# Attended blocks turned on VectorE, and Q and K of two chunks by column-tiled products, in an adaLN block with sliding-window attention and a gated MLP

## The chip, the core and the metric

The kernel runs on one core of a Trainium2 chip. The metric is the device time of one execution in microseconds (us). The engines are TensorE (PE in the profile, its weight loads PEld), VectorE (DVE), ScalarE (ACT), GpSimd (POOL) and SyncE (SP), which issues most of the transfers (DMAs).

## The reference

The input x is 2048 rows of 640, all in bf16. Six vectors of 640 come from the condition c; three modulate the attention branch, three the MLP branch. The attention has 32 heads of 20 columns and a causal window of 256 keys. The MLP is gated, with an inner width of 1536.

```python
mod = (_silu(c) @ w_mod).reshape(c.shape[0], 6, 1, -1)
sa, ca, ga, sb, cb, gb = mod[:, 0], ..., mod[:, 5]

def _A_ref(x, wqkv, wo):            # H = 32, Dh = 20, W = 256
    qkv = (x @ wqkv).reshape(B, S, 3, H, Dh).transpose(2, 0, 3, 1, 4)
    q, k, v = qkv[0], qkv[1], qkv[2]
    scores = jnp.einsum('bhqd,bhkd->bhqk', q, k) * Dh ** (-0.5)
    mask = (i - j >= 0) & (i - j < W)
    p = softmax(jnp.where(mask, scores, -1e9))
    o = jnp.einsum('bhqk,bhkd->bhqd', p, v)
    return o.transpose(0, 2, 1, 3).reshape(B, S, D) @ wo

def _B_ref(x, w_gate, w_up, w_down):
    return (sigmoid(x @ w_gate) * (x @ w_up)) @ w_down

h = _layernorm(x) * (1 + ca) + sa
x = x + ga * _A_ref(h, A_wqkv, A_wo)
h = _layernorm(x) * (1 + cb) + sb
x = x + gb * _B_ref(h, B_w_gate, B_w_up, B_w_down)
```

## The kernel before, in words

The 2048 rows are cut into 8 chunks of 256, each of two blocks of 128. Chunk a goes through these stages.

- `ln1` (L874): load x, LN statistics on DVE (`ln_stats`, L773), the inverse root on POOL, scaling; then the block is turned so that its 640 columns lie on the partitions (hT). Chunks 0 and 1 are turned by TensorE with the identity (`pe_transposes`, L831), the others by a transposing DMA (`transp_dma`, L808). Then scale and shift from the modulation (mA, L766) are applied.
- `qkv` (L917): for Q and K of each block, two halves of 320 columns, each a chain of five products (`pe_chain`, L689) of 128 stationary rows' worth of hT and 320 moving columns of the weight, into one of four PSUM buffers M. `evac` (L899) copies a half to a stage tile stg on ACT or DVE, with every head padded from 20 to 32 columns. The stage tile is then turned to QT or KT, in which a group of four heads lies on the 128 partitions: for chunks 0 and 1 (NPQ = 2) by four products with the identity per half and a copy of 512 columns, for the others by a transposing DMA. V is copied without a turn.
- `attention` (L1176): scores, two halves q of 16 heads each. A set of scores fills the single four-bank PSUM tile S; ACT takes exp of its 2048 columns (L1028, L1054, L1091), POOL masks. Chunk 0 has 6 sets, every other chunk 10. `burst` (L1108) multiplies with V; the row sum is a column of V.
- `norm` (L1146) turns the result on DVE in 32x32 blocks (T, L1150), divides by the row sums into Tn (L1157) and turns it back (On, L1159). Then `close` writes On to a DRAM tensor doc with four DMAs per q and reads oT back from it with one, so that the 640 attended columns lie on the partitions without the padding.
- `outproj` (L1221) multiplies oT with wo, adds to x, takes the second LN and turns it by DMA (h2T). `mlp` (L1275) makes gate and up, tanh on ACT, the product on DVE (hh), then down, the residual and the store. The gates ga and gb are folded into wo (L1331) and wd (L1268).

At the start TensorE warms up with products of zeros (L667, L678) while x and the modulation's weights come in; `load_w3` (L627) loads the weights of Q, K, V by column halves, a first piece of wq ahead of everything else.

The order of the work is not left to a run-time scheduler. Every operation is recorded with its engine choice, its reads and writes and a planned duration; `PLAN` (L353) is a list of numbers written out in the source, each of which names one operation and its engine. `schedule` (L151) takes the operations in this order, gives each tile a buffer by planned times, and `emit` writes every engine's list with semaphore waits. An engine executes its list in order: an instruction that waits holds everything behind it on that engine, and SP's list of transfers works in the same way.

## Time and profile before

| what | us |
|---|---|
| median of 3 runs (lowest, highest) | 326.84 (326.5, 327.2) |
| the profiled execution | 326.74 |
| its span, first to last instruction | 324.8 |
| TensorE busy (5044 products) | 316.1 |
| DVE, ACT, POOL busy | 205.6, 213.0, 188.0 |
| granted TensorE clock | 1.0 throughout |

How to read it: a busy share is an average over the whole span, and products overlap in the array, so that "busy" does not say how many a microsecond holds. The windows give the same by stage, the waits say on whom an engine stood still, the timeline gives starts, and the lines of a group give count, busy time, mean duration in ns and idle time ahead of them. A name such as M<-wk,hT says that M is written from wk and hT; buffer numbers are left out. The four PSUM buffers M are shared by all products but the scores.

### The profile page before, as it was taken

The page shows a single profiled execution, that of the slowest core. Times are in us where ns is not written, and L with a number is a line of the kernel's source. Part 1 is how long each engine was busy: PE and PEld are TensorE (multiplying, and loading weights), DVE is VectorE, ACT ScalarE, POOL GpSimd, SP SyncE. Part 2 cuts the span into 40 slices and gives each one's busy share as a digit, 9 for nine tenths or more (in the row PEclk, how much of TensorE's full clock was granted, in tenths as well). Part 3 has the DMA queues.
Part 4 walks back from the last instruction along what each step waited for, and adds up shares of the span by engine and source line. Part 5 has one row for each costly group of instructions (what it writes and reads, how often), then busy time and mean ns, then how long its engine had stood idle before and what let it go on. Part 6 is the DMA issues. An engine that isn't in the chain of part 4 may idle for free.

```text
span 324.8 us, 11997 instructions
## 1 busy us (share of the span) xinstructions
PE 316.1 (97%) x5044; PEld 236.8 (73%) x5045; DVE 205.6 (63%) x426; ACT 213.0 (66%) x228; POOL 188.0 (58%) x349
## 2 busy tenths in 40 slices
PE   6999999989999999999999999999999999999996
PEld 2666767667776777776787777777888777887885
DVE  4699987768686865674755647464845376645423
ACT  2699984788678877988685857676886756320220
POOL 5337858855868677948774846676583958001000
PEclk9999999999999999999999999999999999999999
DMA  7999989998648464726551303465121206112201
GB/s 238 370 315 245 281 161 189 207 192 281 186 91 140 64 139 75 109 60 130 118 71 26 83 2 73 126 65 120 39 47 28 77 22 83 38 46 41 83 0 42
DMA packets 73023, 38.20 MB, mean 118 GB/s; under 512 B 46602, under 2 KB 71690, under 8 KB 72970
## 3 DMA queue, kind: packets, MB, share of 16 engines
q1 hardware_dynamic: 71808, 36.13, 50.6%
q10 hardware_dynamic: 1162, 1.31, 1.5%
q8 instruction: 40, 0.66, 0.9%
q14 instruction: 13, 0.11, 0.1%
HBM read 21.30 MB, written 5.25 MB: 82 GB/s over the span
## 4 chain that ended last, share of the span: by engine, by line
PE 76%; DVE 0%; issue 0%
PE M L686 64%; PE S L687 6%; PE M L687 5%; DVE x L1306 0%
## 5 line engine op out<-in xcount | busy, mean ns | idle before, releaser
L1054 ACT ACTIVATE E<-S 128x2048 bf16<-128x2048 f32 x56 | 105.0, 1876 | 45.7 <-PE S L687 45.4
L1063 POOL TENSOR_SCALAR_AFFINE_SELECT E<-E 128x512 bf16<-128x512 bf16 x112 | 69.6, 635 | 8.4 <-DVE Tn L1157 2.1
L1059 POOL TENSOR_SCALAR_AFFINE_SELECT E<-E 128x256 bf16<-128x256 bf16 x112 | 45.4, 415 | 48.3 <-PE M L686 14.8
L686 PE MATMUL M<-h2T,wu 128*128 128x256 bf16 x480 | 68.0, 273 | 0.5 <-DVE h2T L828 0.5
L686 PE MATMUL M<-h2T,wg 128*128 128x256 bf16 x480 | 67.0, 273 | 0.0
L686 PE MATMUL M<-wd,hh 128*128 128x320 bf16 (+2 forms) x396 | 57.3, 296 | 0.0
L1287 DVE SCALAR_TENSOR_TENSOR hh<-sig,M 128x512 bf16<-128x512 f32 x48 | 32.2, 680 | 34.9 <-ACT sig L1285 24.1
L686 PEld LDWEIGHTS M<-h2T,wu 128*128 128x128 bf16 x480 | 45.3, 98 | 8.4 <-issue 0.7
L686 PEld LDWEIGHTS M<-h2T,wg 128*128 128x128 bf16 x480 | 45.5, 98 | 6.9 <-DVE T L1150 0.2
L686 PEld LDWEIGHTS M<-wd,hh 128*128 128x128 bf16 x396 | 37.0, 98 | 14.0 <-DVE hh L1287 0.2
L1285 ACT ACTIVATE sig<-M 128x512 f32<-128x512 f32 x48 | 28.2, 596 | 27.7 <-PE M L686 27.1
L1032 POOL TENSOR_SCALAR_AFFINE_SELECT E<-E 128x1024 bf16<-128x1024 bf16 x28 | 31.9, 1144 | 6.8 <-DVE st L781 2.5
L1306 DVE TENSOR_TENSOR x<-M,x 128x320 bf16<-128x320 f32 (+2 forms) x33 | 15.7, 479 | 29.4 <-PE M L686 28.9
L687 PE MATMUL S<-QT,KT 20*64 20x256 bf16 (+5 forms) x1856 | 32.3, 228 | 1.3 <-issue 0.7
L687 PEld LDWEIGHTS S<-QT,KT 20*64 20x64 bf16 (+1 forms) x1856 | 20.0, 100 | 18.4 <-issue 8.8
L781 DVE BATCH_NORM_STATS2 st<-x 128x6 f32<-128x320 bf16 x64 | 28.9, 477 | 1.3 <-DMA x<-in_A_x_dram 1.0
L1150 DVE STREAM_TRANSPOSE T<-M 128x512 f32<-128x512 f32 x32 | 21.4, 698 | 13.1 <-PE S L687 10.5
L1028 ACT ACTIVATE E<-S 128x2048 bf16<-128x2048 f32 x14 | 26.3, 1876 | 5.1 <-PE S L687 5.0
L686 PE MATMUL M<-wq,hT 128*128 128x320 bf16 x160 | 25.9, 300 | 1.5 <-ACT hT L827 0.9
L686 PE MATMUL M<-wv,hT 128*128 128x320 bf16 x160 | 26.8, 300 | 0.0
L686 PE MATMUL M<-wk,hT 128*128 128x320 bf16 x160 | 26.2, 300 | 0.0
L686 PE MATMUL M<-wo,oT 128*128 128x320 bf16 x160 | 24.8, 300 | 0.0
(86 smaller groups left out, 362.7 us busy)
## 6 DMA issues: line engine op xcount, KB each, us to landing
x<-in_A_x_dram SPq DMA_DIRECT2D x19, 160.0 KB, 8.4
doc<-On SPq DMA_DIRECT2D x64, 40.0 KB
out_dram<-x SPq DMA_DIRECT2D x14, 160.0 KB, 1.8
wd<-in_w_mod_dram SPq DMA_DIRECT2D x6, 320.0 KB
wd<-in_B_w_down_dram SPq DMA_DIRECT2D x4, 480.0 KB
wu<-in_w_mod_dram SPq DMA_DIRECT2D x5, 320.0 KB
oT<-doc SPq DMA_DIRECT2D x8, 192.0 KB
wg<-in_B_w_gate_dram SPq DMA_DIRECT2D x2, 576.0 KB
```

Source lines behind the costliest of these rows:

```text
L686: return e.matmul(o, l, r, start=st, stop=sp, skip_group_check=True)
L687: return e.matmul(o, l, r, start=st, stop=sp, tile_position=tp, skip_group_check=True)
L781: A("dve", lambda e, g, bi=bi, j=j: e.bn_stats(v(bi * 12 + j * 6, 6), src[bi].ap[:, j * 320:(j + 1) * 320]), 0.48, reads=[src[bi].r()], wr ...
L1028: A("act", lambda e, eng: e.activation(cell().rearrange("p m (x c) -> p m x c", c=64)[:, :, 0:4:3, :], Sp.ap[:].rearrange("p j (k x c) -> ...
L1032: A("pool", lambda e, eng, c0=c0, pat=pat, base=base, cm=cm: e.affine_select(cell()[:, :, c0:c0 + 64], cell()[:, :, c0:c0 + 64], pattern=p ...
L1054: A("act", lambda e, eng: e.activation(part(0, 512), Sp.ap[:], ACT.Exp, scale=SM_SCALE), 1.876, reads=[Sp.r()], writes=[E.r("C"), E.r("B") ...
L1059: A("pool", lambda e, eng, hc=hc, src=src, far_h=far_h: e.affine_select(side(hc), part(src, 64), pattern=[[0, 4], [-1 if far_h else 1, 64] ...
L1063: A("pool", lambda e, eng, c0=c0, near=near: e.affine_select(part(c0, 128), part(c0, 128), pattern=[[0, 4], [1 if near else -1, 128]], com ...
L1150: A("dve", lambda e, g, h=h: e.transpose(T1.ap[:, 512 * h:512 * h + 512], X[h].ap), 0.694, reads=[X[h].r()], writes=[T1.r(h)], prio=3.5, t ...
L1285: A("act", lambda e, g, pg=pg, sg=sg: e.activation(sg.ap[:], pg.ap[:], ACT.Tanh, scale=0.5), c_act(512), reads=[pg.r()], writes=[sg.r()], ...
L1287: A("dve", lambda e, g, pu=pu, sg=sg, f0=f0: e.scalar_tensor_tensor(out=hh.ap[:, f0:f0 + 2, :], in0=sg.ap[:].rearrange("p (a b) -> p a b", ...
L1306: A("dve", lambda e, g, ps=ps, bi=bi, c0=c0, n=n: e.tensor_tensor(x1[bi].ap[:, c0:c0 + n], ps.ap[:, 0:n], x1[bi].ap[:, c0:c0 + n], op=ALU. ...
```

## The change

1. Attended blocks: doc and its DMAs are gone. Tn is one tile per chunk of 1280 columns without padding (and without its memset on POOL); `norm` divides straight into it, and after the second q two turns on DVE of 640 columns each give oT. This needs another order of heads on the partitions: head 8j + gi where it was 4 gi + j, so wo is loaded with its rows permuted, in five DMAs of one row tile each, and scaled tile by tile.
2. Q and K of chunks 0 and 1: `qk_turned`. hT is the stationary side in pieces of 32 tokens, the weight moves in four pieces of 160 columns side by side in the four column groups of the array. The half is evacuated with padding, and one DVE turn of 128x1024 in 32x32 blocks gives QT or KT. The products with the identity and the copies of 512 columns are gone. The chain of five is cut 1 + 2 + 2.
3. The weights of Q, K, V are loaded by row tiles (1 + 2 + 2 for wq, 3 + 2 for wk and wv) of all 640 columns, behind x and the modulation's weights; chunk 1's x comes between them.
4. A new `PLAN`. Among other things the Q, K and V products of chunk 0 stand together ahead of the first scores, and the first MLP stands further ahead. For the other chunks only the head order changes in the evacuation of Q and K.

Helpers for paired buffers that were switched off (`both`, `both_banks`, PAIR, TR1, PQ) are removed.

```diff
-    p_Tn = sbpool("Tn", 1, [128, 1024])
-    p_On = sbpool("On", 1, [128, 1024])
+    p_Tn = sbpool("Tn", 1, [128, 1280])
...
-    def load_w3(k, prio, halves):
...
+    def load_rows(k, t0, t1, prio):
         i = ("wq", "wk", "wv").index(k)
...
+        dma(lambda: W3[k][:, t0:t1, :], lambda: wqkv_src[:, t0:t1, i * D:i * D + D], 0.44 * (t1 - t0),
+            writes=R_row[k][t0:t1], prio=prio, tag=k)
...
-    dma(lambda: wo[:], lambda: A_wo.rearrange("(t p) f -> p t f", p=128), 2.15, writes=[R_wo], prio=0.5, tag="wo")
+    for t in range(NDT):
+        dma(lambda t=t: wo[:, t, :], lambda t=t: A_wo.rearrange("(j e) f -> j e f", j=4)[:, 32 * t:32 * t + 32, :], 0.43, writes=[R_wo[t]],
+            prio=0.5, tag="wo")
...
+    def qk_turned(a, prio, bi, key, w, dst, s):
+        for half in range(2):
+            ps = Tile(p_M, f"{key}{a}_{bi}{half}")
+            for t0, t1 in CUTS:
+                def fn(e, g, t0=t0, t1=t1, half=half, ps=ps):
+                    for kt in range(t0, t1):
+                        for i in range(2):
+                            k0 = bi * 128 + (2 * half + i) * 32
+                            for j in range(4):
+                                ins = mm(e, ps.ap[32 * j:32 * j + 32, i * 160:i * 160 + 160], hT[a].ap[:, kt, k0:k0 + 32],
+                                         W3[w][:, kt, j * 160:j * 160 + 160], kt == 0 and i == 0, kt == NDT - 1, tp=(0, 32 * j))
+                    return ins
...
+            evac(lambda half=half: s.ap[:].rearrange("p (m b x) -> p b m x", b=4, x=32)[:, 2 * half:2 * half + 2, :, 0:DH],
+                 lambda ps=ps: ps.ap[:, 0:320].rearrange("p (b m d) -> p b m d", b=2, d=DH), 320, [ps.r()], [s.r(half)], 6, f"evqk{a}")
+        A("dve", lambda e, g: e.transpose(dst.ap[:, :, bi * 128:bi * 128 + 128], s.ap[:]), 1.24, reads=[s.r(0), s.r(1)],
+          writes=[dst.r((bi, 0)), dst.r((bi, 1))], prio=5, tag=f"qtr{a}")
...
-                if a < NPQ or (a, key, bi) in PQ:
-                    for half in range(2):
-                        ps = Tile(p_M, "qtr")
...
-                                ins = mm(e, ps.ap[:, i * 128:i * 128 + 128], s.ap[:, gi * 128:gi * 128 + 128], ident[:],
-                                         i == 0, True)
...
-        A("dve", lambda e, g: e.transpose(On.ap[:], Tn.ap[:]), 1.22, reads=[Tn.r()], writes=[On.r()], prio=4, tag=f"tr2_{a}")
+        A("dve", lambda e, g: e.tensor_tensor(
+            Tn.ap[:].rearrange("p (b k d) -> p k b d", k=8, d=DH)[:, 4 * q:4 * q + 4],
+            T1.ap[:].rearrange("p (k b r) -> p k b r", k=4, r=32)[:, :, :, 0:DH],
+            Dr.ap[:].rearrange("p (k b) -> p k b", k=4).unsqueeze(3).to_broadcast([128, 4, 8, DH]), op=ALU.mult),
...
-            for j in range(4):
-                Rj = R(f"doc{a}_{q}_{j}")
-                dma(lambda j=j, q=q: rdoc[j * DH:(j + 1) * DH, 4 * q:4 * q + 4, :],
...
             if q == 1:
+                for bi in range(2):
+                    A("dve", lambda e, g, bi=bi: e.transpose(
+                        oT.ap[:, :, bi * 128:bi * 128 + 128].rearrange("p t (b c) -> p b t c", c=32), Tn.ap[:, 640 * bi:640 * bi + 640]),
+                      0.83, reads=[Tn.r(0), Tn.r(1)], writes=[oT.r(bi)], prio=4, tag=f"tr2_{a}")
                 x1, h2 = outproj(a, oT)
                 mlp(a, x1, h2)
```

130 lines of the change are left out of this document (44 added, 86 removed), and 223 rows, old and new, of the table PLAN.

## The prediction

> **What bounds the kernel now.** I read the page first: busy shares, then the two lines on transfers.
>
> ```profile
> PE 316.1 (97%) x5044; PEld 236.8 (73%) x5045; DVE 205.6 (63%) x426; ACT 213.0 (66%) x228; POOL 188.0 (58%) x349
> DMA  7999989998648464726551303465121206112201
> GB/s 238 370 315 245 281 161 189 207 192 281 186 91 140 64 139 75 109 60 130 118 71 26 83 2 73 126 65 120 39 47 28 77 22 83 38 46 41 83 0 42
> ```
>
> TensorE is busy in 97% of the span and no other engine in more than 66%. The transfers are dense only in the first ten slices, about 80 us. Next come the windows by stage (columns: busy us and count of PE, weight loads, DVE, ACT, POOL; clock; transfer share; GB/s), which say where TensorE is not busy.
>
> ```profile
> 10.00:20.00 10.00, 9.30 (x98) 6.54 (x98) 7.95 (x21) 7.68 (x15) 2.96 (x10) 1.00 1.06 372
> 20.00:30.00 10.00, 9.98 (x173) 6.62 (x172) 9.13 (x25) 9.67 (x10) 7.31 (x12) 1.00 1.05 260
> 30.00:40.00 10.00, 9.73 (x202) 7.20 (x200) 9.35 (x18) 9.42 (x13) 8.35 (x12) 1.00 0.97 266
> 40.00:60.00 20.00, 19.25 (x334) 13.22 (x333) 16.32 (x39) 13.77 (x17) 14.97 (x28) 1.00 1.02 193
> 60.00:80.00 20.00, 18.33 (x328) 13.06 (x326) 14.98 (x33) 16.53 (x20) 11.72 (x21) 1.00 1.09 221
> 200.00:300.00 100.00, 100.00 (x1555) 78.16 (x1553) 56.76 (x108) 56.10 (x53) 53.46 (x97) 1.00 0.33 64
> ```
>
> Between 10 and 80 us TensorE idles 0.70 + 0.02 + 0.27 + 0.75 + 1.67 = 3.41 us; from 80 us on it is always fed, as the last row shows. So from 80 us on only fewer or cheaper TensorE instructions shorten the run, and before that idle time of at most 3.4 us and the start can be won too. But between 20 and 40 us DVE and ACT are over 90% busy: what is put on them there is not free. The waits of TensorE (us in total, times, longest) name who ends that idle time.
>
> ```profile
> PE M L686 <- DVE x L803: 1.3, 1, 1.3
> ...
> PE M L686 <- ACT hT L827: 0.9, 1, 0.9
> PE S L687 <- issue: 0.7, 1, 0.7
> PE M L686 <- DVE h2T L828: 0.5, 1, 0.5
> PE M L686 <- DVE hT L820: 0.5, 1, 0.5
> ```
>
> The reader is to see that no wait on oT, the attended block that comes back from DRAM, is among them. That detour is hidden under other products, so its removal by itself gives TensorE nothing.
>
> **The change part by part.** TensorE's price of an instruction is its distance to the next start, not its modelled duration. These rows of the timeline (start, us, engine, operation) give it:
>
> ```profile
> 25.82 0.67 PEld L687 LDWEIGHTS M<-wu,silubc 128*32 128x32 bf16 x40 [0.21 <-issue]
> 25.83 0.87 PE L687 MATMUL M<-wu,silubc 128*32 128x160 bf16 x40
> 26.63 0.85 PE L686 MATMUL M<-wq,hT 128*128 128x320 bf16 x5
> ...
> 29.08 0.40 PE L686 MATMUL M<-ident,stg 128*128 128x128 bf16 x4
> 29.31 0.84 PE L686 MATMUL M<-wq,hT 128*128 128x320 bf16 x5
> 29.99 0.39 PE L686 MATMUL M<-ident,stg 128*128 128x128 bf16 x4
> 30.31 0.40 PE L687 MATMUL S<-QT,KT 20*128 20x128 bf16 x16
> 30.64 1.53 PE L686 MATMUL M<-wk,hT 128*128 128x320 bf16 x10
> 32.01 0.44 PE L686 MATMUL M<-wv,hT 128*128 128x320 bf16 x2
> ```
>
> *Transposes gone.* Four of them take 29.31 - 29.08 = 0.23 us, 57 ns each. The group row counts 64:
>
> ```profile
> L686 PE MATMUL M<-ident,stg 128*128 128x128 bf16 x64 | 5.6, 220 | 0.0
> ```
>
> All 64 are Q and K of chunks 0 and 1, and all go: 64 x 57 ns = **-3.65 us**.
>
> *Q and K as column-tiled products.* Before: 2 chunks x 2 blocks x 2 (Q, K) x 2 halves x 5 = 80 products of 320 columns, each (32.01 - 30.64) / 10 = 137 ns, 10.96 us. After: each becomes 2 x 4 products of 32 stationary and 160 moving columns, 640 in all. The same form stands at 25.83: 40 of them in 0.80 us, 20 ns each, of which one change of the array's tiling is part. That change costs (30.31 - 29.99) - 0.23 = 0.09 us, so 0.71 / 40 = 17.8 ns, times 640 = 11.4 us: **+0.4 us**. Bounds: at the column rate of the 320-column products, four side by side would take 160 / 320 x 137 = 68.5 ns, 10.96 us in all, so 0; at the full 20 ns it is 12.8 us, +1.85. I take the value of the row itself.
> The Trainium skill, "TensorE: Matmul & The Clock Gate", section "LDWEIGHTS (loading the stationary operand)", gives a load as its columns divided by 1.2 ns. For 32 columns that is an estimate of 27 ns; were every load in line, 640 would make 17.1 us, and the sum would be 5.7 us worse, about 329 us. The trace speaks against it: 40 loads and 40 products together passed in 0.80 us.
>
> *Changes of tiling.* Counting in the two built orders, TensorE changes tiling 170 times before and 175 after (transposes no longer break scores from products, but tiled products stand among 128-wide ones): 5 x 0.09 = **+0.5 us**.
>
> *The start.* At present a 240 KB piece of wq is issued ahead of x and of the five pieces of the modulation; afterwards it stands behind them. These rows are the queue's first issue, the size of that piece, the copy of the finished modulation and the first projection:
>
> ```profile
> 0.79 0.45 SPq L576 DMA_DIRECT2D wq<-in_A_wqkv_dram  x1
> ...
> 10.43 0.17 DVE L766 COPY mA<-S 128x10 f32<-128x10 f32 x1 [1.42 <-PE S L686]
> ...
> 11.32 2.70 PE L686 MATMUL M<-wq,hT 128*128 128x320 bf16 x17 [0.49 <-DVE hT L820]
> ```
>
> ```profile
> wq<-in_A_wqkv_dram SPq DMA_DIRECT2D x1, 240.0 KB
> ```
>
> 240 KB at the 370 GB/s of the second slice are 0.66 us, so modulation and first projection come **0.65 us** sooner (10.65 us). Bounds: 0, if wq's first row then lands last, and 1.1, if the 0.45 us of issue count as well.
>
> *The idle time between 10 and 80 us.* It goes where it is and comes elsewhere. The order is new, so I look for places at which the new one has to wait. One row of scores needs the single S tile, which exp gives back:
>
> ```profile
> 18.61 1.88 ACT L1091 ACTIVATE E<-S 128x2048 bf16<-128x2048 f32 x1
> ...
> 21.01 1.88 ACT L1091 ACTIVATE E<-S 128x2048 bf16<-128x2048 f32 x1
> ...
> 23.44 1.88 ACT L1091 ACTIVATE E<-S 128x2048 bf16<-128x2048 f32 x1
> ```
>
> So sets of scores cannot follow each other faster than every 2.4 us. In the new order there are only 1.4 us of TensorE work between the first and the second set (ten transposes of x, 16 tiled products): 1.0 us of waiting. Rows 3 and 4 of wq: at present 2.21 MB are in some 0.2 us ahead of the copy at 10.43; 2.79 MB, which these rows end, are there 0.58 / 0.37 = 1.6 us later, at 11.8, and TensorE wants them at 10.65 + 0.7: 0.4 us. The products of K find the four buffers of Q still being emptied, all by ACT: 0.4 us. Two later pairs of sets stand 2.0 and 2.2 us apart: 0.6 us. And the first MLP is brought forward: 46.6 us of TensorE work after the first projection where it was 58.0, behind 15 sets of scores instead of 18. It waits for wo, the residual, LN statistics and h2T's turn by DMA:
>
> ```profile
> h2T<-x SPq DMA_TRANSPOSE x16, 5.1
> ```
>
> From the last product of wo (37.4 us into the new order) the adds, statistics and scaling take some 4 us of DVE and POOL, the turn 5.1, the modulation 0.6: 47.1 to 48, so about 1 us late. Together 1.0 + 0.4 + 0.4 + 0.6 + 1.0 = 3.4 us, as much as the 3.41 that is there now: **0**, between -2.4 (all but 1 us goes) and +2.5.
>
> *DVE, ACT and queues.* Rows of DVE's turns, and of the copies that vanish with the transposes:
>
> ```profile
> L1150 DVE STREAM_TRANSPOSE T<-M 128x512 f32<-128x512 f32 x32 | 21.4, 698 | 13.1 <-PE S L687 10.5 <-PE M L687 2.3
> L1159 DVE STREAM_TRANSPOSE On<-Tn 128x1024 bf16<-128x1024 bf16 x16 | 19.9, 1242 | 0.4
> L903 DVE CAST QT<-M 128x512 bf16<-128x512 f32 x5 | 3.4, 683 | 0.3 <-PE M L686 0.3
> L903 DVE CAST KT<-M 128x512 bf16<-128x512 f32 x3 | 2.1, 685 | 0.2 <-PE M L686 0.2
> ```
>
> ```profile
> L902 ACT ACTIVATE KT<-M 128x512 bf16<-128x512 f32 x5 | 3.0, 599 | 0.1
> L902 ACT ACTIVATE QT<-M 128x512 bf16<-128x512 f32 x3 | 1.8, 595 | 0.0
> ```
>
> DVE gets 8 turns of 128x1024, 9.9 us, and loses 5.5 us of copies; ACT loses 4.8. The closing turn shrinks from 1024 to 640 columns, by the first two rows (1.06 ns a column) to 0.83 us, 16 x 0.41 = 6.5 us less, but spread over the run. So in the first 40 us DVE carries 4.4 us more; the order answers by giving ACT the copies of chunk 0. I cost it at nothing on the path, hidden by TensorE's own 8 us of chunk 0 products; if that cover fails, the first scores come late, which is the first rival. The new wait that matters there: DVE's statistics of x2 and x3 stop for their landing (3.77 and 4.42 MB, by the same count about 14.4 and 16.2 us), and behind them stands the turn of K's first block, on which the first set of scores waits; it ends near 18.7, TensorE gets there near 19.7. The 64 writes and 16 reads of the detour leave SP's queue and the transfers; wo comes in 5 row pieces instead of one, the memset of Tn goes. None of these ended a wait of TensorE above: 0.
>
> **Sum.** -3.65 + 0.4 + 0.5 - 0.65 + 0 = -3.4 us. The profiled execution took 326.74 us (324.8 span and 1.94 around it), 0.1 below the median of 326.84; against the median 323.4 us.
>
> **The rivals.**
> 1. *The first 45 us are not TensorE's.* If the chain of copies, turns and exps on ACT and DVE sets the pace there, the 3.65 us of transposes turn into waiting and only the start is won: 326.84 - 0.65 = 326.2, from 325.2 to 327. For it: the 9.1 to 9.7 us of 10 on DVE and ACT. Against: TensorE idles just 0.29 us between 20 and 40 us, and work that it does not do there it does later, always fed. 0.20.
> 2. *The idle time goes.* The MLP's products, available 11 us of work earlier, and a freer queue fill the gaps: 2.4 us less, 321.0. 0.15.
> 3. *Slower: TensorE's instructions don't arrive.* The row
>
> ```profile
> q8 instruction: 40, 0.66, 0.9%
> ```
>
> says 40 fetches for 10089 instructions of TensorE, 252 each, of 0.9% x 16 x 324.8 / 40 = 1.17 us. Now 20 to 40 us needs 747 instructions in 20 us, 37 per us; the tiled Q and K of chunk 0 are 320 products and 320 loads in 5.7 us without a break, one fetch every 2.25 us, while the transfers are saturated. If a fetch may only run one ahead and takes as long as the turn of h2T above (5.1 us), chunk 0 waits 2.5 x 2.85 = 7.1 us: 330.5. The gain of 3.4 us is used up from 2.25 + 3.4 / 2.5 = 3.6 us per fetch on. 0.06.
> The Trainium skill, "Runtime: NRT & Kernel Launch", section "Instruction fetch mechanics", gives TensorE room for 2048 instructions, by which this rival is void, and a few lines on speaks of two blocks only, by which it could hold; no run here shows which.
> 4. *Slower: loads of 32 columns in line*, not beside the products as the 40 of the modulation are, because here the loads bring other columns in turn: 0.67 / 40 = 17 ns each, 640 of them +10.7, 334. 0.03.
>
> **How the numbers follow.** Forecast 0.56 (322 to 325.2), rivals 0.20, 0.15, 0.06, 0.03. Faster by over 0.2% means below 326.2, about what a measurement of this kernel can tell: 0.56 + 0.15 + half of rival 1 = 0.81. Same: 0.08 of rival 1. Slower: 0.06 + 0.03 + 0.02 of rival 1 = 0.11. The range, 320.8 to 326.2, takes in forecast, rival 2 and the lower half of rival 1, and with them the bounds of the tiled products and of the start; 0.19 lies outside.
>
> **What would show it.** Right: 64 fewer products on ident,stg and nothing in their place but 640 tiled ones at about 71 ns per four; first projection near 10.7 us; idle of TensorE between 10 and 80 us near 3.4 us, with one gap of 1 us before the second set of scores and one before the first MLP product; from 80 us no idle time. Wrong: gaps among the tiled products themselves (rivals 3 and 4), DVE's turns late for the first sets of scores (rival 1), or new waits after 80 us, for which I have given no room.

## The result, and the profile after

The changed kernel takes 340.1 us (median of 4 runs, 339.4 to 340.2); the kernel before, run beside it, 326.7 (325.3 to 327.2). The ratio is 1.041, with a 95% interval of 1.038 to 1.045: **slower by 13.4 us** where 3.4 us less were forecast. Two causes make up the difference: TensorE stops for its own instructions among the tiled products, and the five loads of wo run on four of the sixteen transfer engines. Here and below, a time is the median of all runs of a kernel, while a ratio and its interval leave out single runs more than 1.5% above the kernel's fastest (one with wo by strips in the changed kernel, four of the last run).

The profiled execution took 339.4 us, 337.7 of them span. The page of the changed kernel: busy time, clock in 40 slices, fetches of instructions, and the chain that ended last.

```profile
PE 319.5 (95%) x5540; PEld 240.4 (71%) x5541; DVE 197.6 (59%) x410; ACT 213.1 (63%) x234; POOL 189.5 (56%) x350
...
PEclk9979799799999999999999999999999999999999
...
q8 instruction: 43, 0.70, 0.9%
...
PE 93%; issue 4%; ACT 2%; DVE 1%; DVEq 0%; ACTq 0%
```

The kernel before has a granted clock of 1.00 in every window up to 300 us; now three of the first eight slices show 7 tenths, and 4% of the chain is "issue", time in which TensorE waited for nothing that the profile shows. The windows of the changed kernel, columns as in the prediction, say where:

```profile
10.00:20.00 10.00, 5.88 (x241) 5.43 (x242) 4.33 (x10) 2.98 (x8) 0.64 (x3) 0.89 1.01 358
20.00:30.00 10.00, 8.90 (x260) 6.72 (x253) 7.72 (x19) 7.13 (x12) 2.84 (x7) 0.94 0.23 65
30.00:40.00 10.00, 5.44 (x228) 4.18 (x220) 4.63 (x11) 4.63 (x7) 5.79 (x8) 0.91 1.06 219
40.00:60.00 20.00, 17.74 (x356) 11.81 (x344) 15.11 (x29) 14.06 (x18) 9.96 (x14) 0.96 0.88 149
60.00:80.00 20.00, 18.10 (x308) 12.21 (x309) 13.54 (x33) 16.31 (x20) 13.73 (x26) 0.91 0.89 195
80.00:100.00 20.00, 20.00 (x329) 15.39 (x327) 13.58 (x27) 16.52 (x21) 16.62 (x28) 1.00 0.91 229
```

Between 10 and 80 us TensorE idles 4.12 + 1.10 + 4.56 + 2.26 + 1.90 = 13.9 us, 10.5 more than before. The clock column, as the share missing to 1.00 times the window, costs 1.1 + 0.6 + 0.9 + 0.8 + 1.8 = 5.2 us besides. From 80 us on TensorE is fed, as forecast. 10.5 + 5.2 - 3.65 for the transposes that are really gone is 12.1 of the 12.9 us by which the span grew. The timeline of TensorE in the changed kernel (start, us, operation, count, idle time before it and its releaser) shows the stops. These are all its rows with "issue" from the first projection to 55 us:

```profile
11.18 2.77 PE L679 MATMUL M<-wq,hT 128*32 128x160 bf16 x141 [0.66 <-issue]
17.41 0.60 PE L679 MATMUL M<-wq,hT 128*32 128x160 bf16 x19 [3.46 <-issue]
21.79 1.08 PE L679 MATMUL M<-wk,hT 128*32 128x160 bf16 x51 [0.34 <-issue]
32.86 0.23 PE L679 MATMUL S<-QT,KT 20*128 20x128 bf16 x3 [1.70 <-issue]
38.23 0.59 PE L679 MATMUL M<-wk,hT 128*32 128x160 bf16 x11 [2.82 <-issue]
50.88 0.58 PE L678 MATMUL M<-wk,hT 128*128 128x320 bf16 x3 [1.32 <-issue]
```

A stop comes in the middle of a group of products that no semaphore divides: after the 141st of 160 products of Q, for example. Counted from the start, products, loads and TensorE's semaphore instructions together, the five that follow the first row lie exactly behind TensorE's instructions 448, 704, 1216, 1472 and 1984. That is 448 + 256 k. The trace also has each 16384-byte packet of the instruction queue, 64 bytes for each of 256 instructions. Put beside one another, from the trace of the changed kernel (us; "border reached" is the start of the last instruction ahead of a border, "asked for" that of the last instruction ahead of the border before, when the block before is used up; the trace does not show the request itself):

```
border  asked for  packet         border reached  goes on  stop
   448    11.40    14.96-16.03        13.72        17.41   3.70
   704    13.72    19.22-20.30        21.22        21.79   0.57
   960    21.22    22.91-24.08        28.50        28.56   none
  1216    28.50    30.23-31.50        30.94        32.86   1.92
  1472    30.94    35.88-36.98        35.17        38.23   3.05
  1728    35.17    39.66-41.08        45.06        45.22   none
  1984    45.06    48.14-49.34        49.26        50.87   1.61
```

No packet of these comes before the border ahead of its own has been passed, and where TensorE has stopped it goes on 1.25 to 1.53 us after the packet's end. From "asked for" to the packet pass 1.7 to 5.5 us in this stretch. So for TensorE to run on, by this count 256 instructions must last about 1.7 to 5.5 + 1.1 + 1.35 us, 4.2 to 8 us. Counted from "goes on" of the row above instead, it is 1.1 to 3.6 us to the packet, and some 3.6 to 6 us in all; the runs do not tell the two counts apart. Fed, the tiled products go at (13.72 - 11.18) / 141 = 18.0 ns, each with a load: 256 instructions are gone in 2.3 us, under either count too fast. The kernel before crosses the same borders and hardly suffers: its fastest 256 instructions (scores, P V and the tiled modulation from 37.2 us on) take 3.1 us, and behind them it has its one stop, 0.91 us at instruction 1216 (42.84 to 43.75):

```profile
43.75 0.23 PE L687 MATMUL S<-QT,KT 20*64 20x64 bf16 x7 [0.72 <-issue]
```

The clock falls behind a long stop. The trace of the changed kernel in windows of 4 us around the first one (the column before the last two is the clock):

```profile
10.00:14.00 4.00, 3.29 (x153) 2.85 (x151) 2.09 (x8) 2.19 (x6) 0.64 (x3) 1.00 1.07 372
14.00:18.00 4.00, 0.59 (x28) 0.58 (x31) 0.76 (x1) 0.29 (x1) 0.00 (x0) 0.97 1.06 377
18.00:22.00 4.00, 3.66 (x123) 3.46 (x116) 3.18 (x7) 0.93 (x3) 0.14 (x1) 0.61 0.41 153
22.00:26.00 4.00, 4.00 (x80) 2.71 (x69) 2.33 (x4) 2.69 (x7) 1.01 (x4) 1.00 0.02 4
```

0.39 x 4 = 1.6 us more. The same shows at 38 to 42 us, behind the stop of 3.05 us (0.57, 1.7 us more). At 62 to 66 us it is 0.57 again, but behind no stop for instructions: TensorE has just waited 1.29 and 0.60 us for ScalarE. Behind the stops of 1.92 and 1.61 us the windows show 1.00.

### The profile page after: what moved, and what is told of

Its sections match the earlier page's. It is cut to its first block, busy times and chain, and to the rows that moved or that the text cites. A ratio compares the mean times of both kernels' runs of the same rounds, so it can differ in the third digit from the quotient of the medians.

```text
span 337.7 us, 12810 instructions
## 1 busy us (share of the span) xinstructions
PE 319.5 (95%) x5540; PEld 240.4 (71%) x5541; DVE 197.6 (59%) x410; ACT 213.1 (63%) x234; POOL 189.5 (56%) x350
## 4 chain that ended last, share of the span: by engine, by line
PE 93%; issue 4%; ACT 2%; DVE 1%; DVEq 0%; ACTq 0%
PE M L678 71%; PE M L679 11%; PE S L679 8%; PE S L659 1%; ACT E L1007 1%; PE S L678 1%; ACT E L1033 1%; PE S L670 0%; ACT hT L819 0%; DVE h2T L820 0%; DVE hT L858 0%; DVE E L654 0%; DVE x L1274 0%; PE M L643 0%; DVEq L322 0%
## 5 line engine op out<-in xcount | busy, mean ns | idle before, releaser
L1033 ACT ACTIVATE E<-S 128x2048 bf16<-128x2048 f32 x56 | 105.0, 1876 | 37.2 <-PE S L679 36.6
L1038 POOL TENSOR_SCALAR_AFFINE_SELECT E<-E 128x256 bf16<-128x256 bf16 x112 | 46.5, 428 | 54.3 <-ACT E L1033 24.7
L1042 POOL TENSOR_SCALAR_AFFINE_SELECT E<-E 128x512 bf16<-128x512 bf16 x112 | 70.4, 644 | 6.7 <-DVE Tn L1132 3.2
L678 PE MATMUL M<-h2T,wu 128*128 128x256 bf16 x480 | 66.8, 273 | 0.1
L678 PE MATMUL M<-h2T,wg 128*128 128x256 bf16 x480 | 65.5, 273 | 0.0
L678 PE MATMUL M<-wd,hh 128*128 128x320 bf16 (+2 forms) x396 | 58.5, 295 | 0.0
L678 PEld LDWEIGHTS M<-wd,hh 128*128 128x128 bf16 x396 | 37.2, 98 | 13.3
L678 PE MATMUL M<-wv,hT 128*128 128x320 bf16 x160 | 28.2, 313 | 0.0
L894 ACT ACTIVATE stg<-M 128x320 bf16<-128x320 f32 x43 | 17.6, 437 | 16.4 <-PE M L679 10.4
L678 PE MATMUL M<-wo,oT 128*128 128x320 bf16 x160 | 26.1, 300 | 0.0
L679 PE MATMUL M<-E,V 128*32 128x256 bf16 (+1 forms) x960 | 22.7, 246 | 0.8 <-issue 0.8
```

Source lines behind the costliest of these rows:

```text
L678: return e.matmul(o, l, r, start=st, stop=sp, skip_group_check=True)
L679: return e.matmul(o, l, r, start=st, stop=sp, tile_position=tp, skip_group_check=True)
L894: return e.activation(dst(), src(), ACT.Copy)
L1033: A("act", lambda e, eng: e.activation(part(0, 512), Sp.ap[:], ACT.Exp, scale=SM_SCALE), 1.876, reads=[Sp.r()], writes=[E.r("C"), E.r("B") ...
L1038: A("pool", lambda e, eng, hc=hc, src=src, far_h=far_h: e.affine_select(side(hc), part(src, 64), pattern=[[0, 4], [-1 if far_h else 1, 64] ...
L1042: A("pool", lambda e, eng, c0=c0, near=near: e.affine_select(part(c0, 128), part(c0, 128), pattern=[[0, 4], [1 if near else -1, 128]], com ...
```

## The experiments

The theory: TensorE's instructions come in blocks of 256, at most the block in use and the next are there, and the tiled products use them up faster than they come. Rivals: the landing of weight rows, the products and loads of 32 columns as such, the chain of turns and copies on VectorE and ScalarE, the attended blocks, the order. After the first runs a second part came in, the loads of wo. All runs, with the median of each and its ratio to the kernel before, run beside it:

| run | us | ratio [95%] |
| --- | --- | --- |
| changed kernel | 340.1 | 1.041 [1.038, 1.045] |
| Q, K wide, both chunks | 329.3 | 1.010 [1.004, 1.017] |
| Q, K wide, first chunk | 330.5 | 1.013 [1.006, 1.021] |
| Q, K wide, second chunk | 334.8 | 1.027 [1.021, 1.033] |
| before, Q, K in eight tiled products | 337.5 | 1.034 [1.027, 1.040] |
| before, in four | 330.0 | 1.012 [1.006, 1.018] |
| border moved | 338.4 | 1.037 [1.033, 1.041] |
| four transfers under way | 340.4 | 1.044 [1.039, 1.048] |
| attended blocks, order of before, first try | 337.5 | 1.037 [1.032, 1.041] |
| wide with transposes, new order | 342.6 | 1.050 [1.047, 1.053] |
| wide, gate later | 330.7 | 1.012 [1.008, 1.015] |
| attended blocks, second try | 335.2 | 1.026 [1.022, 1.031] |
| changed kernel, wo by strips | 335.9 | 1.027 [1.022, 1.031] |
| wide, wo by strips | 323.1 | 0.989 [0.985, 0.992] |
| attended blocks, wo by strips | 332.9 | 1.020 [1.017, 1.024] |
| before, wo in five loads | 326.9 | 1.002 [0.999, 1.006] |
| before, wo in five loads of four runs | 333.0 | 1.020 [1.016, 1.024] |
| attended blocks, strips early | 329.7 | 1.006 [1.003, 1.010] |

### Q and K by wide products: both chunks, the first, the second

In the changed kernel, for both chunks, or under a condition on the chunk for one of them:

```diff
-                        for i in range(2):
-                            k0 = bi * 128 + (2 * half + i) * 32
-                            for j in range(4):
-                                ins = mm(e, ps.ap[32 * j:32 * j + 32, i * 160:i * 160 + 160], hT[a].ap[:, kt, k0:k0 + 32],
-                                         W3[w][:, kt, j * 160:j * 160 + 160], kt == 0 and i == 0, kt == NDT - 1, tp=(0, 32 * j))
+                        ins = mm(e, ps.ap[:, 0:320], hT[a].ap[:, kt, bi * 128:bi * 128 + 128],
+                                 W3[w][:, kt, half * 320:half * 320 + 320], kt == 0, kt == NDT - 1)
```

> The changed kernel, but each group of eight column-tiled products of the first two chunks' Q, K is one product of 128 x 320 again (560 products and 560 weight loads fewer; the blocks and heads of these Q, K are then no longer those that the later steps take them for, the amount of work of every step is the same). The order, the loads by rows, VectorE's turns of Q, K and the attended blocks on VectorE stay. Theory (TensorE's instructions come in blocks of 256 and are not there in time): the five stops of 10.9 us go, and with them most of the low clock behind them (some 5 us); TensorE is held nowhere for over 0.5 us without a semaphore; 322 to 326 us. Rival (weight rows land too late): the stops stay where the rows land, 337 to 341. Rival (the chain of VectorE's turns and ScalarE's copies sets the first 45 us): 335 to 341, with TensorE waiting on semaphores instead. Rival (the attended blocks on VectorE or the new order cost the time): 338 to 341.

> As before, but only the first chunk's Q, K products are wide; the second chunk's 320 stay tiled. Theory: the stops of the first chunk (3.7 and 0.6 us) go; the second chunk's 320 products and 320 loads use up two and a half blocks of 256 in some 6 us while the transfers are saturated, so one or two stops of 2 to 4 us stay: 327 to 334 us. Rivals as for the first run: 337 to 341.

> As before, but only the second chunk's Q, K products are wide; the first chunk's 320 stay tiled. Theory: the stop near 13.7 us (3.7 us) stays, a second one of 0.5 to 2 us behind it too, those from 30 us on go or shrink: 328 to 334 us. Rivals: 337 to 341.

329.3, 330.5 and 334.8 us. With both wide, no stop is left at a border, and 10.8 of the 13.4 us are gone: the theory holds, and the rivals that leave the tiled products out of it fall as main causes. With the first chunk wide, stops of 2.1 and 3.0 us at the borders 704 and 960 are left, with the second wide 4.0 and 1.4 us at 448 and 704. But 3 us are missing to the range that I gave for both, and the third time lies 0.8 us above its range. TensorE was also to be held nowhere for over 0.5 us without a semaphore, and it waits 1.64 and 4.70 us for "issue", though at no border. The longer one is a new wait. From its timelines, of TensorE, VectorE and GpSimd in turn:

```profile
49.02 1.47 PE L679 MATMUL M<-E,V 128*32 128x256 bf16 x32 [4.70 <-issue]
```

```profile
45.67 0.89 DVE L1296 TENSOR_TENSOR wo<-wo,gbc 128x640 bf16<-128x640 bf16 x2 [5.45 <-DMA gbc<-gate]
```

```profile
48.67 1.15 POOL L1035 TENSOR_SCALAR_AFFINE_SELECT E<-E 128x256 bf16<-128x256 bf16 x3 [9.78 <-DVE wo L1296]
```

TensorE's "issue" is not an instruction block here (the border 1216 lies at 56.95 us). The rows in turn suggest that it waits for masks, GpSimd for VectorE's scaling of wo, and that for the gate's row from DRAM. With the second chunk wide the same wait is 4.5 us.

### The kernel before with tiled products: eight, and four

In the kernel before, each 128 x 320 product of Q, K of chunks 0 and 1 is cut in place; all else, the PLAN too, stays:

```diff
+                    for i2 in range(2) if tiled else ():
+                        for j2 in range(4):
+                            ins = mm(e, o[32 * j2:32 * j2 + 32, i2 * 160:i2 * 160 + 160], l[:, 32 * j2:32 * j2 + 32],
+                                     r[:, i2 * 160:i2 * 160 + 160], k == 0 and i2 == 0, k == len(pairs) - 1, tp=(0, 32 * j2))
```

The second run has one product of all 320 columns for each j2.

> The kernel before, with one edit: each 128 x 320 product of the first two chunks' Q, K is cut into eight column-tiled products of 32 x 160, which give the same numbers at the same place (560 products and 560 loads more). Order, loads, transposes, all other engines stay. Theory: TensorE stops at its 256th-instruction borders among these products, as the changed kernel does, and the clock falls behind the stops: 334 to 342 us. Rival (the loads by rows, VectorE's turns, the attended blocks or the order are what costs): 326 to 329 us.

> The kernel before, with each 128 x 320 product of the first two chunks' Q, K cut into four column-tiled products of 32 x 320 (same numbers at the same place; 240 products and 240 loads more, where the cut in eight added 560 of each). Theory: a block of 256 lasts twice as long among these products (128 products of 35 ns are 4.5 us), so the stops are fewer and shorter: 328 to 333 us, against 337.5 of the cut in eight. Rival (the columns or the loads of 32 cost, whatever the number): 336 us or more. Rival (nothing but the cut in eight hurts): 326 to 327.

337.5 and 330.0 us, both as the theory says. All six stops of over 0.7 us that the run with eight has between 11 and 55 us lie at borders 448 + 256 k (to within one instruction). So the tiled products alone, without any other part of the change, cost 11.7 us in the kernel before, and half their number 2.7. The waits of TensorE (us in total, times, longest) in the run with eight and in the run with four:

```profile
PE M L687 <- issue: 6.7, 5, 3.4
...
PE S L687 <- issue: 1.1, 1, 1.1
```

```profile
PE S L687 <- issue: 1.4, 1, 1.4
...
PE M L687 <- issue: 0.7, 1, 0.7
```

The run with four has the same 32-column loads and the same columns to move, and the clock never falls below 1.00 before 300 us.

### The border moved

In the changed kernel, eight of the products that warm TensorE at the start:

```diff
+    def warm_cut(e, g):
+        for k in range(16):
+            x = 64 * (k % 8)
+            ins = e.matmul(p_S.aps[0][0:32, 3, x:x + 64], Eall[:, 0:32], Eall[:, 128 + x:192 + x], start=True, stop=True)
+        return ins
...
-    o = A("pe", warm if i < 5 else lambda e, g: warm(e, g, 1), 1.03 if i < 5 else 0.52, prio=90, reads=[R_z], extra=wprev, tag="warm", writes=[R("w")])
+    o = A("pe", warm_cut if i < 4 else warm if i < 5 else lambda e, g: warm(e, g, 1), 1.03 if i < 5 else 0.52, prio=90, reads=[R_z], extra=wprev, tag="warm", writes=[R("w")])
```

> The changed kernel with eight of the 512-column products that warm TensorE at the start each written as eight products of 64 columns on 32 partitions (56 products and 56 loads more, before any real work; their result is read by nobody). Theory (blocks of 256 instructions): every border lies 112 of the kernel's own instructions earlier. The stop after the 141st tiled product is no longer there; a stop, if the block isn't there yet, comes after the 85th (shorter than 2 us, since that block is asked for near 7 us), and the next one after the 213th (3 to 5 us, since that block is asked for only when the 85th is past). Time 335 to 343 us, about that of the changed kernel. Rival (weight rows, or a load of 32 columns): the stops stay behind the 141st and the 269th product.

338.4 us, and the stops moved as the count says. The timeline of TensorE in this run:

```profile
11.10 3.30 PE L685 MATMUL M<-wq,hT 128*32 128x160 bf16 x160 [0.66 <-issue]
14.17 1.26 PE L685 MATMUL M<-wk,hT 128*32 128x160 bf16 x53
19.39 3.29 PE L685 MATMUL M<-wk,hT 128*32 128x160 bf16 x107 [3.96 <-issue]
```

All 160 products of Q pass without a stop; it comes after the 53rd product of K, 160 + 53 = the 213th. It is 3.96 us long: the block is asked for at 12.91, its packet is there at 16.95 to 18.05. Where TensorE stops follows the number of instructions ahead of it, not the data. The total hardly changes (a ratio of 1.037 against 1.041, with intervals that overlap): another stop, of 3.22 us, stands at border 1472, and the run moves the stops without measuring their sum.

### Four transfers under way

```diff
-NDMA = 24
+NDMA = 4
```

> The changed kernel with at most 4 transfers under way instead of 24 (each waits until the fourth before it has landed). Theory, with the further step that the packet of instructions queues behind the transfers that are under way: from the use of a block's first instruction to the packet it takes under 3 us in the first 60 us instead of 3.6, 5.5, 4.9, 4.5 and 3.1, and the stops sum to 3 to 8 us instead of 10.9; the time falls to 330 to 339 us unless the loads themselves get slower by as much. Rival (a fetch takes TensorE 4 to 6 us by itself): the distances stay, and the time is 338 us or more.

340.4 us: the further step was not shown. From "asked for" to the packet pass 3.0, 4.0, 2.5, 1.5, 6.0 and 6.0 us, some shorter, some longer, and the stops did not shrink (waits of TensorE in this run, where the changed kernel has 8.1 us in 6 and 1.7 in one):

```profile
PE M L679 <- issue: 10.0, 6, 4.5
PE S L679 <- issue: 2.5, 2, 1.4
```

That a fetch takes longer while transfers are dense stays as an observation: 1.7 to 5.5 us between 11 and 45 us, and at most 1.6 us between 107 and 163 us, in the changed kernel. What holds it up is open.

### The attended blocks and the order, first try; the gate later

Two kernels with the attended blocks and the loads by rows of the change, Q and K by wide products and TensorE's transposes: one in the order of before, one in the new order. A third is the run with wide products with the five codes of wo's scaling moved in PLAN behind the first turn of the attended blocks.

> The attended blocks on VectorE without DRAM and the loads by rows, as the change has them, but the Q, K of the first two chunks by 128 x 320 products and TensorE's transposes as before, and all of it in the order of the kernel before (a few instructions moved where the new layout asks for both halves of a block). Theory: without the tiled products there are no stops but the one of 0.9 us that the kernel before has near 43 us: 323 to 328 us. Rival (the attended blocks on VectorE cost the time): 330 us or more.

> The same parts as in the run of the attended blocks alone, but in the order of the changed kernel (the transposes on TensorE put in soon after the copies that they need), and with the five scalings of wo by the gate moved behind the first turn of the attended blocks, since in the run with wide products these waited 5.5 us for the gate, and masks and TensorE behind them (a stop of 4.7 us). Theory: 329.3 of the wide run, plus 3.65 for the 64 transposes, less 4.7 for that stop and 1 to 3 for the low clock after it: 323 to 329 us. Rival (the new order is what costs): 331 us or more, while the attended blocks alone stay under 328.

> The run with wide products (its Q, K are scrambled as there), with the five scalings of wo by the gate moved on VectorE from behind the first division to behind the first turn of the attended blocks. Theory: the 4.7 us stop of that run is the gate's row landing 8.7 us after its issue, VectorE's scalings waiting 5.5 us for it, GpSimd's masks and TensorE's product with V behind them; it goes, and the low clock after it: 321 to 326 us, so that without the tiled products and without this wait the change is as fast as forecast. Rival (something else of the change, the attended blocks or the order, costs 3 us): 328 us or more.

337.5, 342.6 and 330.7 us: all three missed, in the direction of the rival. The first stops at two borders, 4.8 us at 1216 and 2.5 us at 2240, though it has no tiled products of Q and K: late instructions are not theirs alone. The new order with transposes put into it says little about the order, since TensorE waits there 2.5 us for ScalarE's copies to stg and 4.3 us for the scalings of wo. The third is the instructive one. The scalings no longer wait, yet TensorE stands as long, 3 us later, now behind ScalarE, which waits for a transpose of x by DMA. Its timelines of TensorE and ScalarE:

```profile
52.14 0.66 PE L678 MATMUL S<-QT,KT 20*64 20x256 bf16 x24 [4.82 <-ACT E L1003]
```

```profile
49.73 0.60 ACT L818 ACTIVATE hT<-hT,mA 128x256 bf16<-128x256 bf16 x1 [5.90 <-DMA hT<-x]
```

Moving the one that waits only changes the name of the wait: everything that lands there is late by some 5 us. So the question is what is ahead of it in the transfers.

### The attended blocks, second try

Each half of Q, K now holds the heads that its own transposes need, so the order of before can stay; wo's first load is where the one was, the other four behind the gate's row.

```diff
+                    if a < NPQ:
+                        pairs = [(lambda kt=kt, bi=bi, half=half, ps=ps, w=w: (
+                            ps.ap[:, 0:320].rearrange("p (j x) -> p j x", j=4), hT[a].ap[:, kt, bi * 128:(bi + 1) * 128],
+                            W3[w][:, kt, :].rearrange("p (j x) -> p j x", j=4)[:, :, 80 * half:80 * half + 80])) for kt in range(NDT)]
```

> The attended blocks on VectorE and the loads by rows again, with the Q, K of the first two chunks by wide products and TensorE's transposes, but now each half holds the heads that its own transposes need, so that the order of the kernel before stays as it was on TensorE, ScalarE, VectorE and GpSimd; of the five loads of wo one is issued where the one was, four behind the gate's. Theory (neither the attended blocks nor the rows cost anything; the 11 us of the first try came from its order): 323 to 329 us. Rival (the attended blocks or the rows cost): 333 us or more, as the first try.

335.2 us, again the rival's number. TensorE has one long wait, of 5.3 us, which ends at 53.66. A window of the transfers ahead of it points to the reason (last columns: clock, transfer share, GB/s):

```profile
45.00:48.00 3.00, 3.00 (x45) 2.00 (x44) 0.96 (x3) 0.70 (x1) 0.08 (x1) 1.00 0.26 98
```

Transfers are waiting and yet only 0.26 x 16 = 4.2 engines move data. Of the 223 packets 144 have 1280 bytes, rows of wo, 55 ns each: 4 / 55 ns x 1280 bytes = 93 GB/s. (72 of the others have 1536 bytes and are not rows of wo.) Each of the five loads has as its source four runs of 32 rows, 160 rows apart, `A_wo.rearrange("(j e) f -> j e f", j=4)[:, 32 * t:32 * t + 32, :]`, and 160 KB at 95 GB/s are 1.7 us; five are 8.6 us by this estimate, in which what is issued behind them comes late.

### wo by strips

```diff
-    for t in range(NDT):
-        dma(lambda t=t: wo[:, t, :], lambda t=t: A_wo.rearrange("(j e) f -> j e f", j=4)[:, 32 * t:32 * t + 32, :], 0.43, writes=[R_wo[t]],
+    for j in range(4):
+        dma(lambda j=j: wo[32 * j:32 * j + 32, :, :], lambda j=j: A_wo[160 * j:160 * j + 160, :].rearrange("(t e) f -> e t f", e=32), 0.54,
```

The scalings then wait for all four strips. In the changed kernel, in the run with wide products, and in the second try of the attended blocks:

> The changed kernel, its only edit the load of wo: four loads of 32 partitions by 5 rows each in the place of five loads of 128 partitions by one row (same bytes to the same places). Theory with its second part: while the five loads move, the trace shows 1280-byte packets alone, 4.2 of 16 transfer engines busy and some 95 GB/s, since each load's source is four runs of 32 rows; they take 1.7 us each in the place of 0.43, and the gate's row, the transposes of x and all behind them land 5 to 6 us late. With the strips these stretches go. The stops of TensorE for instructions stay: 334 to 338 us. Rival (the five loads cost nothing): 339 to 341.

> The run with wide products (Q, K scrambled as there) and the load of wo by strips. Theory: without the tiled products and without the slow loads nothing of the change costs: 321 to 326 us, at or under the forecast; no wait of TensorE over 2 us between 10 and 80 us. Rival (the attended blocks or the order cost the 3.5 us): 328 to 330.

> The attended blocks on VectorE with Q, K of the first two chunks by wide products and TensorE's transposes, in the order of the kernel before, as in the second such run, and the load of wo by strips. Theory: what cost 8 us there was the wait of 5.3 us behind the slow loads of wo and the low clock after it, not the attended blocks: 323 to 328 us, level with the kernel before or a little under it. Rival (the attended blocks on VectorE cost): 332 us or more.

335.9, **323.1** and 332.9 us. The first two are as expected. With both costs away the time comes to the 323.4 that was forecast. But this kernel leaves out what its wide products would need: no turn that follows suits them, so the later steps work on other blocks and heads. It measures the costs and replaces nothing.

What the strips save in the changed kernel can be seen in its own trace, with the five loads. Between 52 and 54 us, while the last of them move, 0.27 of the 16 engines work, at 98 GB/s; then ScalarE waits 2.98 us for a transpose of x by DMA, until 58.47, and TensorE for ScalarE's exp:

```profile
60.88 0.43 PE L679 MATMUL S<-QT,KT 20*64 20x256 bf16 x24 [1.29 <-ACT E L1007]
```

This wait, the next one of 0.60 us for hT and the low clock from 62 us on (1.7 us) are not in the trace with strips: 3.6 of the 4.2 us. What TensorE waits for in the changed kernel with strips, and in the wide one with strips:

```profile
PE M L679 <- issue: 8.8, 5, 3.9
PE S L679 <- issue: 1.4, 2, 1.1
PE M L678 <- issue: 1.3, 1, 1.3
```

```profile
PE M L679 <- issue: 1.5, 3, 0.8
PE S L659 <- DVE E L654: 1.3, 1, 1.3
PE M L678 <- DVE hT L858: 0.8, 1, 0.8
```

Of what is over 1 us behind the start, the first has only its stops left and the second nothing (the wait on E is that of the warm-up at 1.3 us). The third run missed: its strips were issued late, all five scalings waited for the last one, and it has a stop of 2.8 us at border 1216, again without tiled products.

### The form of the load in the kernel before, and the strips early

In the kernel before, the one load of wo becomes five at its place, in two forms:

```diff
-    dma(lambda: wo[:], lambda: A_wo.rearrange("(t p) f -> p t f", p=128), 2.15, writes=[R_wo], prio=0.5, tag="wo")
+        dma(lambda t=t: wo[:, t, :], lambda t=t: A_wo[128 * t:128 * t + 128, :], 0.43, writes=[R_wol[t]],
...
+        dma(lambda t=t: wo[:, t, :], lambda t=t: A_wo.rearrange("(j e) f -> j e f", j=4)[:, 32 * t:32 * t + 32, :], 0.43, writes=[R_wol[t]],
```

In the last kernel, two strips go ahead of a piece of the up weights, two to the place of the one load:

> The kernel before with its one load of wo written as five loads of 128 rows each, one run of 128 rows in DRAM per load, all five at the place of the one. Five issues on SyncE in the place of one cost 4 x 0.45 us there. Theory: all 16 transfer engines share each load, as in the one load; 326 to 329 us. Rival (five loads cost by their number): as the next run.

> The same five loads at the same place in the kernel before, but each takes its 128 rows as four runs of 32 rows that lie 160 rows apart, as the changed kernel does (wo's rows are then in another order than this kernel's attended blocks, the amount of work is the same). Theory: 4.2 of 16 transfer engines busy at some 95 GB/s for about 8.5 us in the place of 2.2, the gate's row and the transposes of x behind them late by 5 us or more: 330 to 336 us. Rival (the form of the load doesn't matter): as the run before, 326 to 329.

> The last run of the attended blocks in the order before, with the four strips of wo issued earlier (two ahead of a piece of the up weights, which takes the later place, two where the one load of wo was). There all five scalings waited for the last strip, 3.6 us on VectorE and 4.8 on GpSimd, and a block of instructions was late by 2.6 us. Theory: this was the place of the loads, not the attended blocks: 324 to 329 us. Rival (the attended blocks on VectorE cost): 332 us or more.

326.9, 333.0 and 329.7 us. The first two kernels differ in one line, the source of the loads, and by 6.1 us. Their windows while the loads move, one run first, four runs second:

```profile
33.00:36.00 3.00, 3.00 (x50) 2.11 (x48) 2.77 (x5) 2.94 (x5) 2.73 (x4) 1.00 1.04 293
```

```profile
33.00:36.00 3.00, 3.00 (x51) 2.11 (x49) 2.83 (x5) 2.91 (x5) 2.73 (x4) 1.00 0.28 83
```

And in the second of the two, GpSimd behind the gate's row and TensorE behind VectorE's copy, some ten us after the cause:

```profile
44.83 1.39 POOL L1333 TENSOR_TENSOR wo<-wo,gbc 128x640 bf16<-128x640 bf16 x1 [5.53 <-DMA gbc<-gate]
```

```profile
49.59 2.88 PE L688 MATMUL M<-wv,hT 128*128 128x320 bf16 x12 [4.85 <-DVE stg L905]
```

The Trainium skill, "DMA: Bandwidth & Descriptors", section "Why a DMA increments its semaphore by 16 and not by 1", says that the number of engines is the largest up to 16 that divides the slowest dimension of both sides; for a source of 4 x 32 rows that is 4. The trace agrees, with 0.26 to 0.28 of 16 engines.

The last run, the attended blocks on VectorE in the order of before, comes to a ratio of 1.006 (329.7 us, a little above its range, and its twelve runs lie wide, from 325.7 to 335.2). Most of the 8 us of the second try was thus the form of the loads and their place. Whether the last 2 us are the attended blocks or an order not made for them stays open: no run shows a gain of theirs.

## Why the prediction was wrong, point by point

- *Transposes gone, -3.65.* Nothing speaks against it. None is left, and the wide run with strips, which has neither transposes nor tiled products of Q and K, is 3.5 us faster than the kernel before (0.989 [0.985, 0.992]). That run differs in the loads, the order and the attended blocks too, so the term is not isolated.
- *Tiled products, +0.4.* Right as a price of a product that is there, 18.0 ns against the 17.8 used, and wrong as a price of 640 of them. The working took the duration from 40 products in a row, 80 instructions, too few to outrun a block of 256. The tiled products cost 11.7 us in the kernel before, 12.8 between the two runs with strips (335.9 and 323.1).
- *Changes of tiling, +0.5.* The traces have the 170 and 175 changes that were counted; no run isolates their price.
- *The start, -0.65.* Not borne out by the two traces: the finished modulation was copied at 10.56 (10.43 before), the first projection came at 11.18 instead of 11.32, 0.14 us sooner where 10.65 was forecast. But other traces with the start of the changed kernel have it anywhere from 10.6 to 11.6 us, so the size of this term stays open, and so does what the copy waited for.
- *Idle time between 10 and 80 us, 0, between -2.4 and +2.5.* **The step that failed**: 10.5 us more, and 5.2 us of low clock that has no term at all. The sum took for granted that TensorE's next instruction is always there. The places that I counted came in part (waits on exp of 1.6 us, none before the MLP, whose turn by DMA landed in 2.6 us instead of 5.1), but they are small beside the five stops of 10.9 us. With both costs away, in the wide run with strips, the idle time is 3.3 us, about the 3.4 of the kernel before.
- *Rival 3, instructions that don't arrive, 0.06, 330.5 us.* This happened, and by the mechanism and the break-even that the prediction itself had worked out: 3.6 us for a fetch, and it takes 4.2 to 8 from the asking to the next instruction (3.6 to 6 by the later count). Gaps among the tiled products were its first sign of being wrong, and they came. The price was too low because only the first chunk was counted, and the clock behind the stops (1.6 and 1.7 us) not at all. The chance was too low because I had the rate that was needed, a fetch every 2.25 us, but set no measured fetch against it, only a packet's 1.17 us. The trace of the kernel before had one: 3.8, 2.9 and 3.4 us from "asked for" to the packet at its borders 448, 704 and 1216, before the packet itself. The row that spoke for the rival stood in the list of waits: "issue: 0.7" in the middle of 24 scores. It was the same stop, at border 1216, and I did not ask which instruction it fell on.
- The Trainium skill, "Runtime: NRT & Kernel Launch", section "Instruction fetch mechanics": of its two sentences, the one on two blocks agrees with the borders here (in 7 of 7 rows no packet before the border ahead was passed), the room for 2048 instructions does not.
- *Rival 4, loads of 32 columns in line.* Not so: 141 products with their loads in 2.54 us, 18.0 ns for both, and with half their number most of the cost is gone.
- *Rival 1, VectorE and ScalarE set the first 45 us.* Not seen: with strips and wide products TensorE waits nowhere over 1.3 us. The turns took 1.23 us, as priced.
- *Rival 2, the idle time goes, 321.0 us.* Not so: 13.9 us in the changed kernel, and 3.3 even in the wide run with strips.
- *"wo comes in 5 row pieces instead of one ... 0."* **The second step that failed.** I counted its issues, not on how many engines each would run. 4.2 us in the changed kernel (340.1 and 335.9), 6.2 in the wide one (329.3 and 323.1), 6.1 in the kernel before.
- *The detour gone, 0.* Nothing speaks against it, but no run isolates it.
- The two costs together make the miss: 340.1 with both, 323.1 with neither, 323.4 forecast. They do not simply add up (the strips save 4.2 us with tiled products and 6.2 without). That 323.1 comes so near the forecast is in part luck: the wide run leaves out +0.4 and +0.5 of the sum, and its first projection came at 11.60 us, no sooner than before.

A version that beats both kernels did not come out of this. The 323.1 us are without any turn that suits the wide products; with TensorE's 64 transposes the estimate is 323.1 + 3.65 = 326.8, the time of the kernel before.

## What to carry to other kernels

Count TensorE's instructions per microsecond, loads included, wherever a change makes products smaller: here a block of 256 had to last 4 to 8 us in the loading stage, so a stretch of several hundred instructions at 9 ns apiece (18 for a product with its load) stands still however well its data are timed. A wait named "issue" inside a group of products was here the supply of instructions; at the head of a group it could be something else (the 4.70 us of the first wide run). Find the number of the instruction that it falls on before calling it small. When a load is split or its rows permuted, look at the outermost dimension of its source, and in the trace at a transfer share that stays at a quarter while the queue is full: those who wait for it are others, and later.

## What the runs showed of the hardware that I had not expected

- In the changed kernel TensorE's clock falls to 0.50 for 3.4 us at a time behind a long stop (in the first wide run for 6.8, about its wait of 4.70): 0.61 over the window of 4 us behind the stop of 3.70, 0.57 behind that of 3.05. It stayed at 1.00 with waits of up to 1.4 us (four tiled products) and behind the stops of 1.92 and 1.61 us, but it fell behind the two waits of 1.29 and 0.60 us. The runs give no simple threshold. Each of the two longest stops costs half as much again.
- In the changed kernel none of the seven packets of instructions between 11 and 50 us came before the border ahead of its own was passed, and TensorE needed 1.25 to 1.53 us after a packet's end. In one run (the first try of the attended blocks) a stop at border 1216 ended 4.2 us after the packet's end; why is open.
- While loads whose source is four runs of 32 rows were moving, all transfers together made 83 to 98 GB/s; with loads of a single run of 128 rows, 293 GB/s in the same place of the kernel.
